# Linear attention and two dense layers on one core: five chunks' keys by tokens turned on TensorE instead of loaded, and the list of operations ordered anew

## The chip, the cores and the metric

The kernel runs on one core of a Trainium2 chip. The metric is the device time of one execution in microseconds (us); the time of the kernel before is the median of three runs.

The engines are named as the profile names them: PE is TensorE's matmuls and PEld its weight loads, DVE is VectorE, ACT is ScalarE, POOL is GpSimd, SP is SyncE, whose queue issues the DMAs.

## The reference

The input is q, k and v of shape (2 batches, 8 heads, 768 tokens, 64 features) and one decay `lam` per head. Attention is linear with a decaying state, in blocks of 64 tokens:

```python
intra = einsum('bhic,bhjc->bhij', qb, kb) * Dmask        # Dmask[i, j] = lam ** (i - j) for i >= j, else 0
intra = einsum('bhij,bhjd->bhid', intra, vb)
inter = einsum('bhid,bhde->bhie', qb * lam_pow, kv_state)
out[:, :, sl] = intra + inter
kv_state = lam_block * kv_state + einsum('bhsd,bhse->bhde', kb * rev_pow, vb)
```

The output becomes x, 1536 tokens by 512. Then come two dense layers of the same sizes (512 to 2048 to 512): `g = elu(x @ w_in)`, `x = g @ w_out`, and with other weights `g = softplus(x @ w_in)`, `out = g @ w_out`. All in float32.

## The kernel before, in words

**Attention.** The kernel takes the tokens in 12 chunks of 128 (two blocks of 64), six per batch. For each chunk it loads two tiles of 512 KB: `qk`, q and k by features (a feature per partition, tokens along the row), and `kv`, k and v by tokens (a token per partition, heads and features along the row). So k is loaded twice, in both layouts. The steps of chunk g, with the names that the planner gives them:

- LQ and LV: the loads (`att_load`, L253, and `att_load_kv`, L267). Chunk 0's q and k come in two DMAs of half the columns (L264), all others in one.
- S: the scores, 32 matmuls of 64x64 weights (`att_s`, L293, the matmul is L308) into two PSUM banks `aps`. SC (L325) multiplies them by the decay mask on DVE.
- KP: the keys by tokens times `kdecay`, in place (`att_prep_k`, L281): one instruction of 128x512 on POOL or DVE (L287), or eight of 128x64 on ACT (L285).
- ST: the chunk's contribution to the state, 16 matmuls of these keys against the values (`att_state`, L383, matmul L389). AD (L395, L397) adds it to the decayed state on DVE, and FD (L402) decays the new state for the next chunk.
- QP: q times its powers (L279). X: the outputs, 48 matmuls, 32 in the first chunk of a batch, where there is no state (`att_x`, L331, matmul L339): first the products with the state, then those of the masked scores with the values. XH and XL (L372, L380) split the result into two parts for the dense layers.

**Dense layers.** Products are made of float32 split in a high and a low part, three matmuls each. The first layer's hidden products are `hps` (L412 to L414) and, for two of the three token tiles of 512, a form with seven products instead of eight (`pa`, `pb`, `pd`, on the same lines); the second product of each layer is `y` (L465). Weights come in 64 tasks of 512 KB (`w_load`, L148) and are split by ACT and DVE (L694 to L713).

**The order of the work.** Nothing is ordered by hand. At build time `build` (L618) makes an `Op` for each step, with the engines it may run on and their costs, a key (its due time, counted from the nominal times of `chunk_at`, L625, plus a shift per kind: KQ, KK, KF, KS, KX, KL) and the operations that it depends on. `schedule` (L504) plays these as a list: a free engine takes the ready operation of the lowest key, and the order in which operations are taken is the order of the program. `NUDGE` (L41) shifts the keys of single operations by number. `Q_ON`, `K_ON` and `F_ON` (L598 to L601) say which engines QP, KP and FD may go to. POOL takes an operation only if at least QUEUE operations wait for DVE and DVE is still busy for PACK times POOL's cost (L574 to L578). TensorE takes from three sequences (attention, first products, second products); HELD and PILE (L560) say how many second products must wait before they go ahead of first ones. `FIRST_LOADS` (L604) is the order of SP's first loads. SHIFT (L592) is the chunk from which the scores use one `aps` pair of banks instead of two; the other pair is then given to the sums `y`, so it sets when second products may begin. From chunk JOIN (L594) on, ST is issued inside X. The four PSUM banks b0 to b3 are shared by ST, by the decay powers and by the first layer's products (`take_bank`, L745).

The program opens with 15 matmuls that keep TensorE at work until the first load lands (L189, L192).

Of the kernel before, what the change touches and what calls it, by code (L numbers as in the profile page):

```python
# [13 lines left out]
AF = mybir.ActivationFunctionType  # L14
# [3 lines left out]
P = 128  # L18
# [20 lines left out]


NUDGE = {  # L41
# [6 lines left out]
}  # L48


# [22 lines left out]
def body(ctx, tc, lamc, attqk, attkv, w1, w2, out):  # L73
# [122 lines left out]
    def swapped(p, e):  # L196
        return e ^ p // 2
# [47 lines left out]
    def powers_out(ps):  # L245
        A.activation(out=qpow.rearrange("q a i -> q (a i)"), in_=ps, func=AF.Copy)

    at = {}

    def early(tag):  # L250
        return xp.tile([P, 2, DM], F32, tag=tag, name="early")

    def att_load(g):  # L253
        if g in (3, 4):
            qk = early(("xl2a", "xl2b")[g - 3])
        elif g in (5, 6):
            qk = tq.tile([P, 2, DM], F32, tag=("t1h", "t1l")[g - 5], name="earlyqk")
        else:
            qk = ap3.tile([P, 2, DM], F32, tag="qk", name="qk")
        if g:  # L260
            nc.sync.dma_start(out=qk, in_=attqk[g])
        else:
            for c in (slice(0, HALF), slice(HALF, DM)):
                nc.sync.dma_start(out=qk[:, :, c], in_=attqk[g].rearrange("p (a i) -> p a i", a=2)[:, :, c])  # L264
        at[g] = [qk[:, 0], qk[:, 1]]

    def att_load_kv(g):  # L267
        if g in (2, 3):
            kv = early(("xh2a", "xh2b")[g - 2])
        elif g in (4, 5):  # L270
            kv = tq.tile([P, 2, DM], F32, tag=("t2h", "t2l")[g - 4], name="earlykv")
        else:
            kv = ap2.tile([P, 2, DM], F32, tag="kv", name="kv")
        nc.sync.dma_start(out=kv, in_=attkv[g])
        at[g] += [kv[:, 0], kv[:, 1]]

    def att_prep(e, g):
        q = at[g][0].rearrange("p (a i) -> p a i", a=NPAIR)
# [1 line left out]

    def att_prep_k(e, g):  # L281
        k = at[g][2].rearrange("p (h d) -> p h d", h=H)
        if e == "A":
            for h in range(H):
                A.activation(out=k[:, h], in_=k[:, h], func=AF.Copy, scale=kdecay[:, h:h + 1])  # L285
        else:
            engines[e].tensor_tensor(out=k, in0=k, in1=kdecay.unsqueeze(2).to_broadcast([P, H, D]), op=ALU.mult)  # L287
# [5 lines left out]
    def att_s(g, ps):  # L293
# [13 lines left out]
                x = x.rearrange("q (a i) -> q a i", a=2)  # L307
            T.matmul(out_, k[r, a:a + 64], x, start=True, stop=True, skip_group_check=True)  # L308

        if g:  # L310
            for late_half in range(2):
                for p0 in range(2):
                    for e in range(2):
                        for p in (p0, p0 + 2):
                            mul(p, e, late_half)
        else:
            for p in range(NPAIR):
                for late_half in range(2):
                    for e in range(2):
                        mul(p, e, late_half)  # L320
        sps[g] = ps

# [162 lines left out]
    def Either(on, key, fn, after=(), gate=None, end=None):  # L485
        return Op(on, key, fn, after, gate, end, True)
# [101 lines left out]
    SLIM = 0.72  # L588
    MM3, SCALAR, SB_V, SB_G, PS_V = 0.68, 0.635, (0.69, True), (1.295, True), (0.69, False)
    PIPE = {"P": 0.0, "A": 0.1, "V": 0.08, "G": 0.04, "S": 0.0}  # L590
    PILE, HELD, QUEUE, PACK = 2.9, 3.9, 1, 0.8
    SHIFT = 10  # L592

    JOIN, CHAIN = 99, 99  # L594
    LATENCY, AHEAD = 2.15, 0.0
    FREE = {"P": 4.6, "A": 2.1, "G": 1.4, "V": 1.65, "S": 0.8}
    FIRST, STEP, ATT = 22.4, 4.71, 3.95
    Q_ON = {"V": (0.69, True)}  # L598
    K_ON = {"A": 2.2, "G": (1.04, True), "V": (0.69, True)}
    F_ON = {"G": (0.62, True)}  # L600
    Q_EARLY, K_EARLY, F_EARLY, EASY = {"V": (0.69, True)}, {"G": (1.04, True)}, {"V": (0.415, True)}, 0  # L601
    KQ, KK, KF, KS, KX, KW, KL = 2, 1.01, 1.37, 0.56, 5.54, -0.91, 15.1
    KT, LATE, RAW_LAG, MARGIN = 0.18, 3.1, 0.69, 0.06
    FIRST_LOADS = [("q", 0), ("v", 0), ("q", 1), ("v", 1), ("q", 2), ("v", 3), ("q", 3), ("v", 2), ("q", 4), 1, ("v", 4), 0, ("q", 5), ("q", 6), ("v", 5)]  # L604

    def lkey(name, key):
        return -90.0 + FIRST_LOADS.index(name) if name in FIRST_LOADS else key

# [9 lines left out]
    def build():  # L618
# [133 lines left out]
        def give_bank(ps):  # L752
            banks[owner[id(ps)]] = True
# [5 lines left out]
        def attention_ops():  # L759
# [18 lines left out]
            for g in range(NCHUNK):  # L778
# [5 lines left out]
                    {"S": ("dma", 2.1 if g == 1 else 1.28)}, lkey(("q", g), k - KL), lambda g=g: att_load(g),  # L784
                    get(("S", old_q), ("X", old_q)))
                O["LV", g] = lv = Op(
                    {"S": ("dma", 1.28)}, lkey(("v", g), k - KL + 2.0), lambda g=g: att_load_kv(g),
                    get(("KP", old_v), ("ST", old_v), ("X", old_v)), lambda g=g: g in at)

                box[g] = aps[g % 2 if g < SHIFT else 0]  # L790
# [4 lines left out]
                else:  # L795
                    O["S", g] = s = pe(0.95, k, lambda g=g: att_s(g, box[g]), here)
                if not last:
                    O["KP", g] = Either(K_ON if g > EASY else K_EARLY, k + KK, lambda e, g=g: att_prep_k(e, g), [lv, ends])

                O["SC", g] = sc1 = Op({"V": (0.97, False)}, k + KS, lambda g=g: att_sc(g), [s, spin, O.get(("X", g - 2))])  # L800

# [831 lines left out]
```

## Time and profile before

| | us |
|---|---|
| median of 3 runs | 558.38 (558.3 to 561.29) |
| profiled execution | 559.15 |
| its span in the profile | 557.4 |
| PE busy in the span | 543.0 (97%) |
| DVE busy | 502.5 (90%) |
| ACT busy | 413.5 (74%) |
| POOL busy | 7.8 (1%) |

The profile is of one execution. Its span runs from the first to the last instruction that the profiler saw; 1.75 us of the execution's time lie around it. Times inside the profile are counted from the start of the span. "PEclk" is the clock that was granted to TensorE as a share of 2.4 GHz; its two levels here are 2.4 and 1.2 GHz. "DMA share" is the busy share of the 16 DMA engines. Matmuls are pipelined, so the duration of a single one is longer than the distance to the next; a group's own duration tells what it takes. A wait in square brackets behind an instruction is the idle time of its engine before it, with what ended it; "issue" means that the profile shows nothing that it waited for.

### The profile page before, as it was taken

What the parts mean: (1) busy time and instruction counts of PE and PEld (TensorE: products, weight loads), DVE (VectorE), ACT (ScalarE), POOL (GpSimd) and SP (SyncE); (2) the same over time, 40 slices, a digit from 0 to 9 for tenths busy, and PEclk for the clock granted to TensorE, in tenths of its full rate; (3) what the DMA queues carried; (4) which work ended last, traced back from release to release, by engine and by line L of the source; (5) the groups of instructions that cost most, each with busy time, mean ns of one, the idle gap of its engine ahead of it and who ended that gap; (6) DMA issues with size and microseconds to landing.
All of it is one profiled execution on the core that took longest, in us unless ns stands there. A gap on an engine that the chain in (4) does not pass through costs nothing.

```text
span 557.4 us, 9041 instructions
## 1 busy us (share of the span) xinstructions
PE 543.0 (97%) x3435; PEld 453.2 (81%) x3435; DVE 502.5 (90%) x907; ACT 413.5 (74%) x775; POOL 7.8 (1%) x14
## 2 busy tenths in 40 slices
PE   7799999999999999999999999999999999999997
PEld 6677788888888888888888888888888888888885
DVE  6689999999669996778998999999999999999895
ACT  3569788778577793657767589999876979697881
POOL 1101000000000000000000000000000000000000
PEclk9899999999999999999999999999999999999999
DMA  8958644012024232301310001122121311221023
GB/s 300 408 182 276 200 133 132 2 38 76 1 76 151 77 102 88 113 2 38 113 54 24 1 1 38 39 81 71 38 76 38 115 38 47 67 79 36 1 94 133
DMA packets 14987, 49.87 MB, mean 89 GB/s; under 512 B 1760, under 2 KB 2272, under 8 KB 14944
## 3 DMA queue, kind: packets, MB, share of 16 engines
q1 hardware_dynamic: 14800, 49.29, 26.0%
q8 instruction: 27, 0.44, 0.4%
q14 instruction: 16, 0.13, 0.1%
q10 hardware_dynamic: 144, 0.01, 0.0%
HBM read 46.15 MB, written 3.15 MB: 88 GB/s over the span
## 4 chain that ended last, share of the span: by engine, by line
PE 87%; DVE 7%; ACT 2%; issue 1%; DMA 1%; SPq 0%; DVEq 0%; ACTq 0%
PE y L465 44%; PE pa L413 5%; PE pa L412 5%; PE pa L414 5%; PE hps L412 3%; PE hps L413 3%; PE hps L414 3%; PE aps L339 3%; PE pd L413 2%; PE pd L414 2%; PE pd L412 2%; DMA qk<-attqk 1%; PE pb L413 1%; PE pb L414 1%; PE pb L412 1%
## 5 line engine op out<-in xcount | busy, mean ns | idle before, releaser
L465 PE MATMUL y<-woh,g 128*128 128x512 f32 x384 | 118.7, 390 | 0.0
L465 PE MATMUL y<-g,woh 128*128 128x512 f32 x384 | 118.5, 390 | 0.0
L992 ACT ACTIVATE g<-v 128x512 fp32r<-128x512 f32 x96 | 60.0, 627 | 38.5 <-PE y L465 33.6
L465 PEld LDWEIGHTS y<-g,woh 128*128 128x128 f32 x384 | 71.9, 188 | 15.0
L465 PEld LDWEIGHTS y<-woh,g 128*128 128x128 f32 x384 | 71.2, 188 | 14.2
L610 DVE TENSOR_TENSOR g<-v,g 128x512 fp32r<-128x512 f32 x96 | 65.5, 686 | 10.3 <-ACT g L992 10.0
L465 PE MATMUL y<-g,wol 128*128 128x512 f32 x192 | 74.7, 389 | 0.0
L465 PE MATMUL y<-wol,g 128*128 128x512 f32 x192 | 74.7, 389 | 0.0
L1343 DVE TENSOR_TENSOR yacc<-y,yacc 128x512 f32<-128x512 f32 x68 | 44.6, 685 | 8.8 <-PE y L465 8.7
L694 ACT ACTIVATE r<-raw 128x512 f32<-128x512 f32 x64 | 42.4, 663 | 5.2 <-DMA raw<-w 3.1
L475 ACT ACTIVATE e<-e 128x512 f32<-128x512 f32 x72 | 45.0, 626 | 0.8
L708 DVE CUSTOM_DVE_ANT_0 r<-r,c 128x1024 uint16<-128x1024 uint16 x64 | 43.8, 684 | 1.3 <-ACT c L698 0.2
L698 ACT ACTIVATE c<-raw 128x512 uint32<-128x512 uint32 x64 | 42.4, 663 | 2.3 <-DVE r L708 2.3
L465 PEld LDWEIGHTS y<-wol,g 128*128 128x128 f32 x192 | 36.0, 188 | 7.5
L465 PEld LDWEIGHTS y<-g,wol 128*128 128x128 f32 x192 | 36.0, 188 | 7.5
L967 ACT ACTIVATE e<-e 128x512 f32<-128x512 f32 x48 | 30.0, 626 | 9.8 <-DVE e L964 9.5
L610 DVE TENSOR_TENSOR e<-e,e 128x512 f32<-128x512 f32 x48 | 32.6, 683 | 2.3 <-ACT e L967 2.1
L964 DVE SCALAR_TENSOR_TENSOR e<-e,e 128x512 f32<-128x512 f32 x48 | 32.7, 683 | 1.3 <-ACT e L958 1.3
L412 PE MATMUL hps<-xh,wih 128*128 128x512 f32 x80 | 31.7, 396 | 0.0
L413 PE MATMUL hps<-xl,wih 128*128 128x512 f32 x80 | 31.2, 390 | 0.0
L414 PE MATMUL hps<-xh,wil 128*128 128x512 f32 x80 | 31.1, 389 | 0.0
L958 ACT ACTIVATE e<-e 128x512 f32<-128x512 f32 x48 | 30.0, 625 | 0.5
(228 smaller groups left out, 1194.2 us busy)
## 6 DMA issues: line engine op xcount, KB each, us to landing
raw<-w SPq DMA_DIRECT2D x64, 512.0 KB, 3.7
kv<-attkv SPq DMA_DIRECT2D x8, 512.0 KB, 5.7
qk<-attqk SPq DMA_DIRECT2D x7, 512.0 KB, 7.7
out<-yacc SPq DMA_DIRECT2D x12, 256.0 KB, 2.1
early<-attqk SPq DMA_DIRECT2D x2, 512.0 KB, 9.6
early<-attkv SPq DMA_DIRECT2D x2, 512.0 KB, 9.7
earlykv<-attkv SPq DMA_DIRECT2D x2, 512.0 KB, 10.6
earlyqk<-attqk SPq DMA_DIRECT2D x2, 512.0 KB, 11.0
```

Of the source, the lines that this page charges most:

```text
L412: T.matmul(ps, wh[:, wo[i]], xa[i], start=(start and i == 0), stop=False, skip_group_check=True)
L413: T.matmul(ps, wh[:, wo[i]], xb[i], start=False, stop=False, skip_group_check=True)
L414: T.matmul(ps, wl[:, wo[i]], xa[i], start=False, stop=(stop and i == n - 1), skip_group_check=True)
L465: T.matmul(yps[m], a, b, start=(begins(key) and i == 0), stop=(ends(key) and i == 2))
L475: A.activation(out=o, in_=a, func=AF.Exp, scale=-1.0)
L610: engines[e].tensor_tensor(out=o, in0=a, in1=b, op=ALU.subtract)
L694: A.activation(out=r, in_=high.bitcast(F32), func=AF.Prelu, scale=2.0 ** -112, alpha=-2.0 ** 32)
L698: A.activation(out=box["c"], in_=box["low"], func=AF.Copy, scale=2.0 ** -29)
L708: V.tensor_tensor(out=ri, in0=ri, in1=box["c"], op=ALU.add)
L964: V.scalar_tensor_tensor(out=e, in0=box["u"], scalar=-1.0, in1=e, op0=ALU.add, op1=ALU.subtract)
L992: A.activation(out=g[:, 0], in_=box["v"], func=AF.Copy)
L1343: V.tensor_tensor(out=y, in0=yps[m], in1=y, op=ALU.add)
```

## The change

- For chunks 0 to 4 (`g < TURN`), the keys by tokens are no longer loaded: `att_load_kv` loads the values alone, 256 KB. The new `att_turn` makes the keys from those by features: 16 matmuls per chunk, each of a 64x64 block of k as weights against the 64x64 identity `ids`, into two PSUM banks. It is an operation of TensorE with S as its dependency, a key of 0.43 after S's, and the condition that at least two of the four shared banks are free. KP of these chunks reads PSUM and writes the tile in SBUF: two instructions of 128x256 on DVE, or eight of 128x64 on ACT, not on POOL. The banks come free when KP has run.
- Chunk 0's q and k are loaded by one DMA, and its scores are issued in the order of the other chunks.
- The planner's numbers are new: where QP, KP and FD may run (POOL now for QP, no longer for KP or FD), the shifts of the keys, HELD, QUEUE and PACK, FIRST and STEP, the order of the first loads, SHIFT from 10 to 8, JOIN from 99 to 8 (so ST of chunks 8 on goes inside X), and all of NUDGE (52 operations shifted before, 71 after).

```diff
 NUDGE = {
-    338: -0.7, 340: -0.4, 344: 0.2, 353: 0.0, 356: 0.9, 360: -5.0, 362: 1.4, 364: 3.1, 373: 0.3, 384: -4.1, 387:
...
+    159: 8.7, 339: 3.1, 344: -9.3, 347: -3.3, 356: -1.1, 361: -0.1, 379: -3.9, 489: -10.1, 500: -2.4, 509: 4.6,
...
-    at = {}
+    at, turned = {}, {}
...
+    TURN = 5
...
-        if g:
-            nc.sync.dma_start(out=qk, in_=attqk[g])
-        else:
-            for c in (slice(0, HALF), slice(HALF, DM)):
-                nc.sync.dma_start(out=qk[:, :, c], in_=attqk[g].rearrange("p (a i) -> p a i", a=2)[:, :, c])
+        nc.sync.dma_start(out=qk, in_=attqk[g])
...
-        nc.sync.dma_start(out=kv, in_=attkv[g])
+        if g < TURN:
+            nc.sync.dma_start(out=kv[:, 1], in_=attkv[g][:, DM:2 * DM])
+        else:
+            nc.sync.dma_start(out=kv, in_=attkv[g])
         at[g] += [kv[:, 0], kv[:, 1]]
+
+    def att_turn(g, ps):
+        k = at[g][1]
+        for half in range(2):
+            for p0 in range(2):
+                for e in range(2):
+                    r = slice(64 * e, 64 * e + 64)
+                    for p in (p0, p0 + 2):
+                        c = 64 * (swapped(p, e) ^ half)
+                        a = P * p + 64 * half
+                        T.matmul(
+                            ps[e][c:c + 64, D * p:D * p + D], k[r, a:a + 64], ids[r], start=True, stop=True,
+                            skip_group_check=True)
...
     def att_prep_k(e, g):
         k = at[g][2].rearrange("p (h d) -> p h d", h=H)
-        if e == "A":
+        if g < TURN:
+            for c, ps in enumerate(turned[g]):
+                if e == "A":
+                    for p in range(NPAIR):
+                        h = 2 * p + c
+                        A.activation(out=k[:, h], in_=ps[:, D * p:D * p + D], func=AF.Copy, scale=kdecay[:, h:h + 1])
+                else:
+                    V.tensor_tensor(
+                        out=k[:, c::2], in0=ps[:, 0:NPAIR * D].rearrange("p (a d) -> p a d", a=NPAIR),
+                        in1=kdecay[:, c::2].unsqueeze(2).to_broadcast([P, NPAIR, D]), op=ALU.mult)
+        elif e == "A":
...
-    PILE, HELD, QUEUE, PACK = 2.9, 3.9, 1, 0.8
-    SHIFT = 10
-    JOIN, CHAIN = 99, 99
+    PILE, HELD, QUEUE, PACK = 2.9, 6.9, 4, 0.0
+    SHIFT = 8
+    JOIN, CHAIN = 8, 99
...
-    FIRST, STEP, ATT = 22.4, 4.71, 3.95
-    Q_ON = {"V": (0.69, True)}
-    K_ON = {"A": 2.2, "G": (1.04, True), "V": (0.69, True)}
-    F_ON = {"G": (0.62, True)}
-    Q_EARLY, K_EARLY, F_EARLY, EASY = {"V": (0.69, True)}, {"G": (1.04, True)}, {"V": (0.415, True)}, 0
-    KQ, KK, KF, KS, KX, KW, KL = 2, 1.01, 1.37, 0.56, 5.54, -0.91, 15.1
-    KT, LATE, RAW_LAG, MARGIN = 0.18, 3.1, 0.69, 0.06
-    FIRST_LOADS = [("q", 0), ("v", 0), ("q", 1), ("v", 1), ("q", 2), ("v", 3), ("q", 3), ("v", 2), ("q", 4), 1, ("v", 4), 0, ("q", 5), ("q", 6), ("v", 5)]
+    FIRST, STEP, ATT = 22.28, 4.76, 3.95
+    Q_ON = {"G": (1.295, True), "V": (0.69, True)}
+    K_ON = {"A": 2.2, "V": (0.69, True)}
+    F_ON = {"V": (0.415, True)}
+    Q_EARLY, K_EARLY, F_EARLY, EASY = {"G": (1.295, True), "V": (0.69, True)}, {"G": (1.04, True)}, {"V": (0.415, True)}, 0
+    KQ, KK, KF, KS, KX, KW, KL = 1.54, -2.34, 1.37, 0.56, 5.54, 1.23, 15.1
+    KN = 0.43
+    KT, LATE, RAW_LAG, MARGIN = 0.84, 3.1, 0.5, 0.09
+    FIRST_LOADS = [("q", 0), ("v", 0), ("q", 1), ("q", 2), ("v", 1), ("v", 3), ("q", 3), ("v", 2), ("q", 4), 1, ("v", 4), 0, ("q", 5), ("q", 6), ("v", 5)]
...
                 if not last:
-                    O["KP", g] = Either(K_ON if g > EASY else K_EARLY, k + KK, lambda e, g=g: att_prep_k(e, g), [lv, ends])
+                    k_on, here, give = K_ON if g > EASY else K_EARLY, [lv, ends], None
+                    if g < TURN:
...
+                        k_on = {e: (0.78, False) if e == "V" else t for e, t in k_on.items() if e != "G"} or {"V": (0.78, False)}
+                        here = here + [pe(0.5, k + KN, turn, [s], lambda: sum(banks.values()) > 1)]
+                    O["KP", g] = Either(k_on, k + KK, lambda e, g=g: att_prep_k(e, g), here, end=give)
```

## Rows read from the trace of the kernel before

**Rows 1.** The page's parts 1 and 3: TensorE's busy time, DMA queue 8 (packets, MB, share).

```profile
PE 543.0 (97%) x3435; PEld 453.2 (81%) x3435; DVE 502.5 (90%) x907; ACT 413.5 (74%) x775; POOL 7.8 (1%) x14
...
q8 instruction: 27, 0.44, 0.4%
```

**Rows 2.** Windows by stage: length, busy us (instructions) of each engine, PEclk, DMA share, GB/s.

```profile
4.83:11.55 6.72, 4.53 (x114) 3.75 (x113) 3.73 (x10) 2.59 (x8) 1.04 (x1) 1.00 1.00 392
11.55:19.36 7.81, 7.30 (x219) 6.25 (x219) 5.56 (x10) 4.57 (x17) 0.62 (x1) 1.00 1.03 410
19.36:21.87 2.51, 0.00 (x2) 0.01 (x2) 1.47 (x3) 2.51 (x8) 1.00 (x1) 1.00 0.99 395
21.87:27.67 5.80, 5.70 (x126) 5.00 (x127) 3.31 (x6) 1.01 (x3) 0.73 (x1) 0.71 1.03 412
27.67:28.91 1.24, 0.00 (x0) 0.00 (x0) 1.24 (x3) 0.98 (x2) 0.00 (x0) 1.00 1.02 403
28.91:30.63 1.72, 1.64 (x55) 1.44 (x55) 1.25 (x3) 0.55 (x2) 0.00 (x0) 1.00 1.04 398
30.63:75.00 44.37, 42.74 (x698) 34.63 (x692) 41.19 (x71) 36.74 (x83) 3.75 (x4) 1.00 0.59 194
75.00:550.00 475.00, 473.68 (x2203) 396.15 (x2203) 438.69 (x786) 363.22 (x659) 0.00 (x0) 1.00 0.19 62
550.00:557.40 7.40, 3.69 (x17) 2.73 (x15) 2.73 (x4) 0.00 (x0) 0.00 (x0) 1.00 0.38 142
```

**Rows 3.** TensorE's timeline, 4.8 to 30 us: start, duration, group [idle before].

```profile
4.83 1.53 PE L308 MATMUL aps<-qk 64*64 64x128 f32 x32
...
7.73 1.40 PE L339 MATMUL aps<-sc,kv 64*64 64x64 f32 x32 [0.34 <-DMA kv<-attkv]
8.94 0.85 PE L308 MATMUL aps<-qk 64*64 64x128 f32 x32
11.55 0.90 PE L308 MATMUL aps<-qk 64*64 64x128 f32 x32 [1.75 <-DMA qk<-attqk]
...
18.80 0.56 PE L389 MATMUL stps<-early 128*64 128x64 f32 x11
21.87 0.39 PE L389 MATMUL stps<-early 128*64 128x64 f32 x5 [2.51 <-issue]
...
27.17 0.50 PE L339 MATMUL aps<-sc,earlykv 64*64 64x64 f32 x9
28.91 1.11 PE L339 MATMUL aps<-sc,earlykv 128*64 128x64 f32 x23 [1.24 <-issue]
```

**Rows 4.** DMA queue 8 in the windows 12 to 33, 19 to 20 and 26 to 27 us.

```profile
q8 instruction: 4, 0.07, 1.2%
...
q8 instruction: 1, 0.02, 6.3%
...
q8 instruction: 1, 0.02, 6.4%
```

**Rows 5.** Groups by line and shape, 0 to 60 us: key and state scaling, state addition, q.

```profile
L285 ACT ACTIVATE kv<-kv,kdecay 128x64 f32<-128x64 f32 x32 | 8.0, 335 | 0.4 <-DMA kv<-attkv 0.4
...
L402 POOL TENSOR_TENSOR faded<-state,qpow 128x256 f32<-128x256 f32 x7 | 6.1, 872 | 40.1 <-DVE state L397 21.4 <-DVE state L395 12.0 <-ACT early L285 6.6
...
L279 DVE TENSOR_TENSOR qk<-qk,qpow 128x512 f32<-128x512 f32 x6 | 4.1, 678 | 0.0
...
L397 DVE TENSOR_TENSOR state<-stps,faded 128x256 f32<-128x256 f32 x7 | 2.9, 415 | 0.1
...
L279 DVE TENSOR_TENSOR early<-early,qpow 128x512 f32<-128x512 f32 x2 | 1.8, 894 | 0.0
...
L287 POOL TENSOR_TENSOR kv<-kv,kdecay 128x512 f32<-128x512 f32 x1 | 1.0, 1044 | 6.4 <-DMA kv<-attkv 6.4
```

**Rows 6.** TensorE's timeline at 52.55 us: the outputs of a chunk, held by q's multiplication.

```profile
52.55 0.67 PE L339 MATMUL aps<-qk,state 64*64 64x128 f32 x16 [0.99 <-DVE qk L279]
```

More of the change, by code (lines that the diff above doesn't have):

```diff
@@ L308, in mul @@
             T.matmul(out_, k[r, a:a + 64], x, start=True, stop=True, skip_group_check=True)
[L310 to L319, printed above, removed]
+        for late_half in range(2):
+            for p0 in range(2):
+                for e in range(2):
+                    for p in (p0, p0 + 2):
                         mul(p, e, late_half)
@@ L786, in attention_ops @@
                 O["LV", g] = lv = Op(
-                    {"S": ("dma", 1.28)}, lkey(("v", g), k - KL + 2.0), lambda g=g: att_load_kv(g),
+                    {"S": ("dma", 0.64 if g < TURN else 1.28)}, lkey(("v", g), k - KL + 2.0), lambda g=g: att_load_kv(g),
                     get(("KP", old_v), ("ST", old_v), ("X", old_v)), lambda g=g: g in at)
@@ L797, in attention_ops, with turn, give @@
                 if not last:
-                    O["KP", g] = Either(K_ON if g > EASY else K_EARLY, k + KK, lambda e, g=g: att_prep_k(e, g), [lv, ends])
+                    k_on, here, give = K_ON if g > EASY else K_EARLY, [lv, ends], None
+                    if g < TURN:
+                        def turn(g=g):
+                            turned[g] = [take_bank("turned") for e in range(2)]
+                            att_turn(g, turned[g])
+                        def give(g=g):
+                            for ps in turned[g]:
+                                give_bank(ps)
+                        k_on = {e: (0.78, False) if e == "V" else t for e, t in k_on.items() if e != "G"} or {"V": (0.78, False)}
+                        here = here + [pe(0.5, k + KN, turn, [s], lambda: sum(banks.values()) > 1)]
+                    O["KP", g] = Either(k_on, k + KK, lambda e, g=g: att_prep_k(e, g), here, end=give)
                 O["SC", g] = sc1 = Op({"V": (0.97, False)}, k + KS, lambda g=g: att_sc(g), [s, spin, O.get(("X", g - 2))])
```

12 rows, old and new, of the table NUDGE are left out of this document.

## The prediction

> **What bounds it now.** I read the page first, then the windows by stage, then TensorE's timeline of the start, then the DMA queues. Everything is set against the profiled execution: 559.15 us, a span of 557.4 us and 1.75 us around it. The median of the three runs shown, 558.38, is 0.77 below, so I subtract that from every sum. About 0.5% (2.8 us) is what a measurement of this kernel can tell from no change, so "faster" means below 555.6 and "slower" above 561.2.
>
> TensorE is busy for 543.0 of 557.4 us [rows 1]. The windows say where the other 14.4 us lie [rows 2]: from 75 to 550 us it is idle for only 475.00 - 473.68 = 1.3 us, from 30.63 to 75 for 1.6, in the tail for 3.7 (last sums and stores, which the change does not touch). The stretch from 4.83 us (the first chunk's scores) to 30.63 (the first matmul of the first layer) holds 6.6 us of idleness: 2.2 + 0.5 + 2.5 + 0.1 + 1.2 + 0.1 over its six windows. One of these windows also ran at a mean granted clock of 0.71 of 2.4 GHz, that is partly at 1.2 GHz, right after TensorE had stood for 2.51 us; against full speed that is 5.80 x 0.29 = 1.7 us lost. So 8.3 us are to be had at the start and hardly anything elsewhere. In all six windows the DMA engines are full (share 0.99 to 1.04).
>
> What are those waits? The timeline [rows 3] names loads for two: 0.34 us for the first keys and values, 1.75 us for chunk 2's q and k. The two longest, 2.51 and 1.24 us, have no releaser. Both fall inside a group whose members share their operands (after 11 of 16 state products, after 9 of 32 output products), and between them lie exactly 5+32+16+48+16+9 = 126 matmuls. Queue 8 carries instructions: 27 packets, 0.44 MB, so 16 KB each; TensorE executes 2 x 3435 = 6870 instructions, 254 for each packet, 127 matmuls with their weight loads [rows 1]. Between 12 and 33 us there are four such packets, one of them at each stop [rows 4]. I read both stops as TensorE standing at the end of a code block whose successor has not come. From stop's end to stop's end it is 28.91 - 21.87 = 7.04 us. Counting 127 back from 19.36 gives 14.75, 7.1 us before 21.87; another 127 back is S(1) at 8.94. So with full DMA engines TensorE gets one block of 127 matmuls per 7 us, while such a block needs only about 7.30/219 x 127 = 4.2 us.
>
> **The change, part by part.**
>
> *Turns.* Five chunks get 16 matmuls each, 64 x 64, as heavy as the second halves of the scores. S(1) does 32 in 0.85 us [rows 3], so a turn is 0.43 us and five are **+2.1**. Lower bound 0, if all lie in load waits; upper bound by code: 80 of 127 matmuls x 7.04 = +4.4. I take 2.1: as long as code paces TensorE, 160 more instructions leave it 80 matmuls behind when transfers thin out, and it makes these up at full speed. A turn waits for what S(g) waits for, and for two free banks. Behind it in TensorE's order stand the state products; banks bind only once layer-one products want one, after 30 us.
>
> The Trainium skill (Runtime: NRT & Kernel Launch, "Instruction fetch mechanics") says code comes in 16 KiB blocks of 256 instructions, fetched while the current one runs, so that crossing a boundary is mostly hidden. The block size agrees with the rows; "mostly hidden" does not for the two stops of 2.51 and 1.24 us. By that rule the waits would be for loads alone; that is the first rival.
>
> *Loads.* Five loads of keys and values shrink from 512 to 256 KB: 1.31 MB, at 403 to 410 GB/s [rows 2] 3.2 us of transfer. Chunk 0's values land 0.64 us earlier, so X(0) and S(1), at the beginning of a code block, move up: **-0.5** (0 to -0.64). Chunk 2's q and k have 768 KB less ahead of them, 1.9 us, and their 1.75 us wait goes; but S(2) lies in the same code block, so what it gains is stood off at the next boundary: 0 in the sum (-1.75 as a bound). The transfers end 3.2 us earlier, near 27.4 us, which is where the second stop begins; I take that stop as gone, **-1.24** (0 to -1.24).
>
> *First load whole.* One issue on SyncE instead of two, nothing late behind it. S(0) ran 1.53 us instead of S(1)'s 0.85, so it waited for the second half inside; whole, it starts later and ends about where it did. 0, bounds -0.5 and +0.5.
>
> *Scaling of keys.* Before: POOL 1.04 us for chunk 0, ACT 8 x 0.335, or DVE. After: ACT as before, or DVE twice 128x256 from PSUM; the nearest row, the state addition from PSUM, takes 0.415 [rows 5], so 0.83. Fades move from POOL (0.87) to DVE at about that 0.415. Five scalings and four fades are 5.8 us on DVE at most; it is idle for 25.8 - 16.6 = 9.2 us in the stretch, so 0. Without that cover the state chain would be late by one 0.83.
>
> *List anew.* Multiplications of q may go to POOL when DVE has four jobs waiting. A DVE row beside POOL averages 894 ns instead of 678 [rows 5]; DVE has 3.2 us of slack between 30.63 and 75, so 0, bound +1. The 0.99 us stop at 52.55, for a q multiplication behind others on DVE [rows 6], should go with new keys: **-1.0** (0 to -1.0). Products that join outputs from chunk 8 are only reordered. With one score bank for chunks 8 to 11, S(g) waits for the split of chunk g-1, while output products may start two chunks earlier; TensorE has both to pick from: 0, at worst +1. From 75 us on the new shifts can win or lose the 1.3 us that stand idle there: 0, bounds -1.3 and +1.3.
>
> Sum: 2.1 - 0.5 - 1.24 - 1.0 = -0.6; 558.5 against the profiled execution, **557.7** against the median. From the bounds, this case reaches from 555.6 to 561.
>
> **Rivals.**
>
> *Loads were the bound all along.* If the code arrives in time once the engines carry less, or if the new order brings boundaries to where TensorE waits anyway, then the start is left with TensorE's own work. All of it is 8.3 us of loss gone against 2.1 of turns: -6.2, 552.2. With half the loss left it is 4.15 - 2.1 = -2.05, 556.3 before later gains and 555.3 with the 1.0 above. I put it at 554.2. For it: the first 0.34 and 1.75 us are loads by name, and everything from chunk 1 on arrives 0.6 to 3.2 us earlier. Against: the two largest stops name no load.
>
> *A third stop, slower.* After the second stop the kernel needs only 55 matmuls to the first long one [rows 2], so the next boundary falls among matmuls of 128x512, where 127 take 27 us (475 us for 2203 from 75 us on); it costs nothing. Eighty more matmuls make it 135, over the 127 of a block: the third boundary falls among the small ones. If the transfers are still full there, the stop is 7.04 - 4.2 = 2.8, and no stop goes: 2.1 - 0.5 + 2.8 = +4.4, 562.8; with 1.7 of half clock after it, 564.5. It is decided by whether the share of the DMA engines is still near 1 when that boundary comes. Against: 3.2 us less transfer.
>
> *It does not do what it says.* The outputs need the values and the q's as before; if keys were never the last to land, no wait goes and only the turns stay. That gives +2.1, 560.5, inside the first case's bounds, and I count it there.
>
> **Chances.** Code pace with the saving eaten, 557.7: 0.45, all of it "same". Loads as the bound, 554.2: 0.38, faster; the queue's 3.2 us is a large saving against 2.1 us of matmuls, and half of these can lie in waits. Third stop, 562.8: 0.17, slower. The range from 553.0 to 562.0 leaves out the end of the second case (0.07) and most of the third (0.11). The first case's own range is 555.6 to 561.
>
> **What would show it.** Right: 3515 matmuls; chunk 2's scores about 2 us earlier; queue 8's packets still some 7 us apart up to 27 us, with stops without a releaser inside groups, the first of them now with less old work done; the first layer-one product within 1.5 us of 30.6. The first rival shows no such stop over 1 us and layer one beginning before 28. The second shows three stops, or a granted clock under 0.8 over more than 6 us, and layer one beginning after 33. Wrong in another way would be idle time of TensorE of over 3 us between 75 and 550 us, or a longer tail: then the list, not the keys, sets the difference.

## The result, and the profile after

The changed kernel takes 564.22 us (median of 5 runs, 563.69 to 564.73). The kernel before takes 560.08 in 5 runs on the same chip, and the ratio of the two sets of runs is 1.0078 with a 95% interval of 1.0054 to 1.0101: slower by 3 to 5.7 us. On another chip, with twelve runs of the kernel before, it came to 1.0088 (1.0075 to 1.0101). The forecast was 557.7 with a range up to 562.0.

| | before | after |
|---|---|---|
| profiled execution, us | 559.15 | 564.41 |
| its span | 557.4 | 562.7 |
| PE busy | 543.0 | 547.6 |
| PE matmuls | 3435 | 3595 |
| MB moved by the DMA engines | 49.87 | 48.58 |

The page's parts 1 and 3 of the kernel after, the lines that answer to [rows 1]:

```profile
PE 547.6 (97%) x3595; PEld 456.5 (81%) x3595; DVE 501.3 (89%) x911; ACT 414.7 (74%) x780; POOL 2.0 (0%) x7
...
q8 instruction: 28, 0.46, 0.3%
```

TensorE executes 160 matmuls more, not the 80 that I had priced, and one more packet of code is fetched. The windows by stage show where the time went; the cuts are at the stops, as in [rows 2]:

```profile
4.83:12.36 7.53, 7.36 (x207) 5.97 (x206) 6.11 (x21) 1.59 (x4) 0.00 (x0) 1.00 1.01 398
12.36:14.27 1.91, 0.00 (x1) 0.00 (x1) 1.17 (x3) 1.35 (x7) 0.00 (x0) 1.00 1.02 403
14.27:17.96 3.69, 3.60 (x126) 3.25 (x127) 1.83 (x3) 2.59 (x10) 0.00 (x0) 1.00 1.01 406
17.96:20.55 2.59, 0.00 (x1) 0.00 (x0) 1.18 (x3) 1.36 (x3) 0.00 (x0) 0.88 1.02 403
20.55:30.44 9.89, 9.71 (x253) 8.66 (x253) 7.19 (x14) 4.27 (x14) 1.28 (x1) 0.69 0.84 324
30.44:31.99 1.55, 0.00 (x0) 0.00 (x0) 1.17 (x3) 1.55 (x7) 0.00 (x0) 1.00 0.00 0
31.99:34.13 2.14, 2.05 (x55) 1.71 (x55) 1.60 (x3) 0.62 (x2) 0.00 (x0) 1.00 0.04 11
34.13:80.00 45.87, 45.23 (x730) 36.14 (x724) 39.84 (x73) 35.18 (x73) 0.00 (x0) 1.00 0.53 185
80.00:130.00 50.00, 49.10 (x224) 39.96 (x221) 48.91 (x94) 41.09 (x75) 0.00 (x0) 1.00 0.20 64
...
400.00:550.00 150.00, 147.97 (x742) 125.84 (x741) 144.26 (x260) 120.67 (x224) 0.00 (x0) 1.00 0.19 62
550.00:562.70 12.70, 8.83 (x39) 6.97 (x38) 6.82 (x11) 1.90 (x3) 0.00 (x0) 1.00 0.28 105
```

The first layer-one product starts at 34.13 us instead of 30.63, and chunk 5's scores (0.9 us), which the kernel before had done by then, are still to come: 4.4 us behind. There are three stops without a releaser, 6.05 us together, against 3.75 before. Between the first two lie 126 matmuls, as between the two stops before; between the second and the third 253, two blocks. The third stop, at 30.44, comes when the DMA engines are empty (share 0.00). The granted clock was 0.69 over 9.89 us, a loss of 3.1 us against 1.7 before.

Summed over these windows, TensorE is idle for 6.6 us between the first scores and the first layer-one product, as long as before (29.30 - 22.72 and 25.80 - 19.17). The stops have taken the place of the waits for data. So the 4.4 us are busy time: 1.4 of half clock, and some 3 us of turns.

After that the list shows in both directions. From the first product to 80 us TensorE is idle for 0.64 us (1.63 up to 75 us before), so the stop at 52.55 [rows 6] is gone: -1.0. From 80 to 550 us it is idle for 0.90 + 2.03 = 2.9 us (1.3 from 75 on before): +1.6. The tail has 3.87 instead of 3.71. Sum: 4.4 - 1.0 + 1.6 + 0.2 = 5.2; the spans differ by 5.3.

TensorE's timeline of the start, which answers to [rows 3]:

```profile
7.91 0.69 PE L291 MATMUL turned<-ids,qk 64*64 64x64 f32 x32
...
11.23 0.69 PE L291 MATMUL turned<-ids,qk 64*64 64x64 f32 x32
11.74 0.61 PE L336 MATMUL aps<-qk 64*64 64x128 f32 x14
14.27 0.54 PE L336 MATMUL aps<-qk 64*64 64x128 f32 x14 [1.91 <-issue]
...
20.55 0.48 PE L411 MATMUL stps<-early 128*64 128x64 f32 x4 [2.59 <-issue]
...
31.99 0.45 PE L411 MATMUL stps<-earlykv 128*64 128x64 f32 x7 [1.55 <-issue]
```

A turn is 32 matmuls and 0.69 us here. A float32 matmul stands in the profile twice: the 16 that the code writes for a turn are 32 in these rows, as the 16 of the scores are 32 and the 8 of `att_state` 16. (The description of the kernel before counts scores, outputs and state products as the profile does, but the turns as the code does.) The group behind the second turn begins 0.51 us after it (11.23 to 11.74), so counted to the next group a turn can take less than 0.69. The waits for loads (0.34 and 1.75 us) are gone, as forecast, and chunk 2's scores begin at 11.74, no earlier than the 11.55 of before.

### The profile page after: what moved, and what is told of

It is laid out like the page before. It is cut to its first block, busy times and chain, and to the rows that moved or that the text cites. A ratio compares the mean times of both kernels' runs of the same rounds, so it can differ in the third digit from the quotient of the medians.

```text
span 562.7 us, 9348 instructions
## 1 busy us (share of the span) xinstructions
PE 547.6 (97%) x3595; PEld 456.5 (81%) x3595; DVE 501.3 (89%) x911; ACT 414.7 (74%) x780; POOL 2.0 (0%) x7
## 2 busy tenths in 40 slices
DMA packets 14588, 48.58 MB, mean 86 GB/s; under 512 B 1744, under 2 KB 1744, under 8 KB 14544
## 4 chain that ended last, share of the span: by engine, by line
PE 94%; DVE 2%; issue 2%; DMA 1%; ACT 0%; DVEq 0%
PE y L487 46%; PE pa L434 5%; PE pa L435 5%; PE pa L436 5%; PE aps L361 4%; PE hps L434 3%; PE hps L435 3%; PE hps L436 3%; PE pd L435 2%; PE pd L436 2%; PE pd L434 2%; PE aps L336 2%; PE pb L435 1%; PE pb L434 1%; PE pb L436 1%
```

## The experiments

Three theories stood against each other. **Code pace**: TensorE gets its code in blocks of 256 instructions, slowly while transfers run, so the turns' instructions cost. **Work**: the turns cost the 5 x 0.69 = 3.5 us that TensorE spends on them. **List**: the new order costs.

**1. Taking the turns out, or putting them alone into the kernel before.** The changed kernel with whole loads and no turns, operation numbers kept so that each shift meets its operation, and chunk 0's keys scaled on DVE as in the changed kernel:

```diff
-    TURN = 5
+    TURN = 0
...
```

> The changed kernel without its turns: the five chunks' keys by tokens are loaded as before (512 KB instead of 256), scaled on ACT or DVE, and the new list, its shifts and its other rules stay. Theory code pace: the turns are 160 of TensorE's matmuls with their loads, 320 instructions, one and a quarter code blocks, so without them the start has two stops without a releaser instead of three, the first layer-one product comes near 30.5 to 31.5 us instead of 34.1, and the time is 560 to 561. Rival work alone: the turns cost what their matmuls take, 5 x 0.69 = 3.5 us, so about 560.7, but with stops as long as in the changed kernel (6.0 us together). Rival new list: the loss is in the order and the shifts, the time stays at 563 or more.

Measured: 1.0133 (1.0117 to 1.0149), slower than the changed kernel. The first product came at 31.28 us, 2.9 earlier, with chunk 5's scores already done. But the list, planned for the turns, came out in another order without them. TensorE's waits in that run's window from 80 to 130 us grew from 0.9 to 3.4 us, 2.34 of them one wait for a sum on ACT. So the run shows that taking the turns out speeds up the start, and nothing of the total. The turns alone in the kernel before, with the old list:

```diff
-        nc.sync.dma_start(out=kv, in_=attkv[g])
+        if g < TURN:
+            nc.sync.dma_start(out=kv[:, 1], in_=attkv[g][:, DM:2 * DM])
...
+                        here = here + [pe(0.5, k + KN, turn, [s], lambda: sum(banks.values()) > 1)]
```

> The kernel before with the turns alone: same list, same rules and shifts, first load in halves, five chunks' keys turned and their loads halved. Theory code pace: as many instructions at the start as the changed kernel, so three stops of 5 us or more together, first layer-one product at 33 to 35, time 3 to 5 us over the kernel before (563 to 565). Rival work alone: +2 to +3.5. Rival new list: the time of the kernel before or less, 558 to 560.

Measured: 1.0161 (1.0143 to 1.0178), +9 us, more than any theory gave. Stops of 1.89, 1.52, 0.84 and 1.49 us, the first product at 35.10, and at 58.47 a wait of 2.28 us for scaled keys on DVE. With turns, the new list is thus the better one: 4.1 to 4.9 us over the kernel before instead of 9. Since the planner makes another order when operations are taken out or added, the order is held fixed from here on, and only what is issued inside an operation changes.

**2. The same order with little code, and with no turns.** The turn as 2 matmuls of 256 columns:

```diff
-        for half in range(2):
...
+        for e in range(2):
+            r = slice(64 * e, 64 * e + 64)
+            T.matmul(
+                ps[e][:, 0:NPAIR * D].rearrange("p (a d) -> p a d", a=NPAIR), k[r, 0:P],
+                ids[r].unsqueeze(1).to_broadcast([64, NPAIR, D]), start=True, stop=True, skip_group_check=True)
```

> The changed kernel with each turn made by 2 matmuls of 256 columns in place of 16 of 64 (4 for 32 as the profile counts them): about the same time on TensorE (2 x 256 columns of float32 for 16 x 64, half the columns, but no cover of two array halves at once: 0.5 to 0.9 us a turn against 0.69), and 280 instructions fewer. It leaves out the turning: every head gets the first head's keys. Theory code pace: the stops stand where the instructions of the kernel before would put them, two instead of three or three with the third among layer-one products, first layer-one product at 30.5 to 32, time 560.5 to 562. Rival work alone: nothing changes, 564 within 1. Rival new list: nothing changes either.

And no matmul at all in the turn's place, the scaling reading `ids`:

> The changed kernel in its own order, without one matmul of the turns: the loads stay halved, the scaling of the keys reads the identity in SBUF instead of the turned keys in PSUM (it leaves out the turning, so the keys are the identity's). Theory code pace: TensorE's instructions at the start are those of the kernel before, so two stops without a releaser in place of three, at the 256-instruction marks of that order; against the kernel with 2 matmuls a turn only the 0.7 us of each turn go, and only where no stop swallows them: 0 to 3.5 us less than its 563.0, so 559.5 to 562.5. Rival work alone: the turns' matmuls (3.5 us) and nothing else, so 560.7 with the stops unchanged at 6 us. If the halved loads are worth the 3.2 us of transfer that they save, the first layer-one product comes 3 us before the 30.6 of the kernel before.

Measured: 1.0065 (1.0043 to 1.0086) and, on another chip, 1.0011 (0.9996 to 1.0027). To divide the loss, all three were run side by side:

> The changed kernel itself, again, so that it stands on one chip and beside the same runs of the kernel before as the two variants that follow. 1.0065 to 1.009 of the kernel before.

> The changed kernel with 2 matmuls of 256 columns a turn, again (TensorE is as long at each turn, 0.70 us for 0.69, with 280 instructions fewer; it leaves out the turning). Theory code pace: 0.3 to 0.5% less than the changed kernel. Theory work: less than 0.15% below it.

> The changed kernel without a matmul of the turns, again (the keys are the identity's). Theory work: 0.5 to 0.65% less than the kernel with 2 matmuls a turn, the 3.5 us that TensorE no longer spends. Theory code pace: within 0.2% of it, since both have nearly the same instructions.

| | turns on TensorE | instructions of the turns | ratio to before (95%) |
|---|---|---|---|
| as changed | 5 x 0.69 us | 320 | 1.0088 (1.0075 to 1.0101) |
| 2 matmuls a turn | 5 x 0.70 us | 40 | 1.0066 (1.0049 to 1.0082) |
| none | 0 | 0 | 1.0031 (1.0019 to 1.0043) |

The step for the code is 0.22% (1.2 us; the intervals just overlap), the step for the work 0.35% (2.0 us; they don't), and 0.31% (1.7 us) is left without any turn. Neither theory alone holds. Three limits belong to this table. The kernel without turns had come to 1.0011 on the other chip, so what is left without turns is 0.1 to 0.3%. Taking the turn out also takes out the scaling's wait for it, and the scaling reads SBUF instead of PSUM; the runs do not separate this from the time of the matmuls. And without turns TensorE stands for 3.6 us in waits for DVE between 4.83 and 30.16 us, so part of the turns had filled such waits.

The timeline of the kernel with 2 matmuls a turn, in the run beside the other two, shows what the code does: two stops, 3.68 us, and none between the second and layer one:

```profile
8.02 0.70 PE L286 MATMUL turned<-ids,qk 64*128 64x256 f32 x4
...
16.08 0.87 PE L356 MATMUL aps<-sc,kv 128*64 128x64 f32 x14 [1.39 <-issue]
...
22.93 0.26 PE L331 MATMUL aps<-early 64*64 64x64 f32 x1 [2.29 <-issue]
...
32.87 0.50 PE L429 MATMUL hps<-xh,wih 128*128 128x512 f32 x1
```

The changed kernel's second profile, from this run, shows how far the stops vary from one execution to the next. Its windows at the stops:

```profile
19.56:20.46 0.90, 0.00 (x2) 0.00 (x0) 0.86 (x3) 0.90 (x2) 0.00 (x0) 1.00 1.05 419
20.46:24.64 4.18, 3.79 (x127) 3.15 (x126) 3.73 (x8) 2.17 (x7) 0.00 (x0) 1.00 1.03 411
24.64:26.64 2.00, 0.01 (x1) 0.00 (x0) 0.77 (x2) 1.30 (x7) 0.00 (x0) 1.00 0.99 397
26.64:30.29 3.65, 3.55 (x126) 3.20 (x127) 2.92 (x6) 0.84 (x3) 1.28 (x1) 1.00 0.53 210
30.29:30.47 0.18, 0.00 (x2) 0.00 (x1) 0.18 (x2) 0.18 (x2) 0.00 (x0) 1.00 0.00 0
```

With the first, again of 1.91 us, these are four stops, one at each count of 126 or 127 matmuls, 4.99 us together. The first layer-one product comes at 32.61 and the span is 562.2, against 34.13 and 562.7 in the first profile. The counts are the same, the lengths aren't. Queue 8 shows what ends a stop. These are its rows of the first profile, in the windows 11.7 to 11.8, 18.1 to 18.2 and 29.6 to 29.7 us, where the packets ahead of the three stops start:

```profile
q8 instruction: 1, 0.02, 67.6%
...
q8 instruction: 1, 0.02, 66.8%
...
q8 instruction: 1, 0.02, 60.0%
```

The stops end at 14.27, 20.55 and 31.99, each 2.3 to 2.6 us after its packet starts, the last one too, though the other transfers are over by then. In the second profile packets start at 12.0, 18.1, 24.2 and 28.1, and the four stops end 2.4 to 2.5 us later. So a stop is long when its packet starts late, or when TensorE has used up the block before it early. What sets the start of a packet was not settled.

The second profile also tells which terms of the first belong to that execution alone. Its start, the stretch to 80 us and the one behind it:

```profile
4.83:32.61 27.78, 21.32 (x642) 18.11 (x641) 19.74 (x47) 13.28 (x43) 1.28 (x1) 0.94 0.87 341
32.61:80.00 47.39, 45.73 (x739) 36.43 (x733) 41.10 (x74) 35.06 (x73) 0.00 (x0) 1.00 0.53 179
80.00:550.00 470.00, 467.16 (x2173) 390.44 (x2173) 432.71 (x777) 363.04 (x660) 0.00 (x0) 1.00 0.19 61
```

At the start TensorE is idle for 6.5 us and loses 1.7 to the clock, both as in the kernel before, and it is 2.9 us behind (2.0, and chunk 5's scores): that is what the turns take. Up to 80 us it is idle for 1.7 us, no less than before, 0.94 of it in two waits for DVE, one of them again for a multiplication of q. From 80 to 550 us it is idle for 2.8 us, +1.5, and the tail is 0.2 longer. That makes 4.6; the spans differ by 4.8. So the extra half clock and the gain at 52.55 us are not to be counted on, while the turns and the waits behind 80 us are in both profiles.

**3. What the halved loads are worth.** The kernel before in its own order, the five loads halved, no turning:

```diff
+        if g < 5:
+            nc.sync.dma_start(out=kv[:, 1], in_=attkv[g][:, DM:2 * DM])
...
+        x = ids.unsqueeze(1).to_broadcast([P, H, D]) if g < 5 else k
```

> The kernel before in its own order, with the five loads of keys and values halved and no turning: the scaling of the keys reads the identity in SBUF (it leaves out the keys by tokens of five chunks). TensorE's instructions are those of the kernel before. It measures what 3.2 us less transfer are worth where they cost nothing. Theory loads as the bound: 2 to 3.2 us faster than the kernel before, first layer-one product near 28. Theory code pace and chain of data: the stops stay at the same matmuls (behind 11 of chunk 3's state products, behind 9 of chunk 4's output products), only the 1.75 us wait for chunk 2's q and k goes, and most of it is stood off at the next stop: within 1 us of the kernel before.

Measured: 0.9990 (0.9972 to 1.0008), no difference that can be measured. Its timeline:

```profile
10.40 0.90 PE L312 MATMUL aps<-qk 64*64 64x128 f32 x32 [0.89 <-DMA qk<-attqk]
...
14.37 0.99 PE L343 MATMUL aps<-sc,kv 128*64 128x64 f32 x19 [0.33 <-issue]
...
21.21 0.39 PE L393 MATMUL stps<-early 128*64 128x64 f32 x5 [2.30 <-issue]
...
27.50 1.11 PE L343 MATMUL aps<-sc,earlykv 128*64 128x64 f32 x23 [1.32 <-issue]
...
29.22 0.50 PE L416 MATMUL hps<-xh,wih 128*128 128x512 f32 x1
```

Both stops stand behind the same 11 and 9 matmuls as in [rows 3] and are about as long as before, though they end 0.7 and 1.4 us earlier. A third, of 0.33 us, stands 126 matmuls ahead of the first: the boundary that the prediction had counted back to 14.75, which cost nothing in the kernel before. 3.2 us of transfer saved give 1.4 us in this profiled execution and about 0.5 in the median; the interval allows 1.6 at most. In this order, then, the loads were not the bound.

**4. What is left: the list.** This kernel and the one without turns have the same instructions of TensorE at the start and the same loads; they differ in the list (and in the first load, and the two profiles in the clock: 1.000 and 0.993 on average, 3.9 us over the span, so the spans are not compared). Their windows from 80 to 130 and from 400 to 550 us, first the old list, then the new:

```profile
80.00:130.00 50.00, 50.00 (x222) 41.44 (x221) 49.64 (x94) 38.92 (x71) 0.00 (x0) 1.00 0.18 62
...
400.00:550.00 150.00, 148.70 (x731) 125.46 (x730) 142.62 (x256) 116.48 (x213) 0.00 (x0) 1.00 0.18 60
```

```profile
80.00:130.00 50.00, 49.19 (x216) 40.08 (x215) 49.78 (x96) 41.31 (x74) 0.00 (x0) 1.00 0.21 67
...
400.00:550.00 150.00, 147.96 (x736) 125.49 (x735) 144.27 (x259) 119.58 (x221) 0.00 (x0) 1.00 0.19 61
```

TensorE idles 2.85 us in these with the new list and 1.30 with the old: +1.55, and the waits are the changed kernel's, whether turns run or not. In the changed kernel they are, from 80 to 130 and from 400 to 550 us:

```profile
PE pa L434 <- DVE v L1167: 0.8, 1, 0.8
```

```profile
PE y L487 <- DVE wol L633: 1.2, 1, 1.2
PE za L434 <- DVE v L1240: 0.8, 1, 0.8
```

All three are for DVE, which is 98 and 96% busy there. Which shift or rule makes each was not tried.

**5. Moving the block boundaries.** If the stops are ends of code blocks, more instructions ahead of all work must move them by as many matmuls. Five kernels issue more, smaller matmuls at the opening:

```diff
-        for n, times in ((256, 5), (384, 2)):
+        for n, times in ((32, 64), (256, 1), (384, 1)):
```

> The changed kernel with the opening matmuls cut smaller: 64 of 32 columns in place of 5, so 59 matmuls (118 instructions) more ahead of the first scores, in the time when TensorE waits for its first load anyway. Theory code blocks: each stop moves by 59 matmuls back in the order of work (the first from the 14th of chunk 2's scores to the 3rd or so of chunk 0's state products, the second from the 12th of chunk 2's state products to the first output products of chunk 1); the time stays within 1.5 us of the changed kernel's, since the pace of the blocks is the same. Rival, the stops are waits for data that the profile does not name: they stay behind the same matmuls.

```diff
-        for n, times in ((256, 5), (384, 2)):
+        for n, times in ((256, 2),):
...
+        for i in range(34):
+            T.matmul(ps[:64, :64], zero[:64, :64], zero[:64, :64], start=True, stop=True)
```

> The changed kernel with 68 small matmuls (64x64) in place of 5 of the opening ones, 63 matmuls or 126 instructions more ahead of the first scores, for about the same time on TensorE (earlier than 5.5 us). Theory code blocks: each stop moves 63 matmuls back in the order of work: the first from inside chunk 2's scores to the beginning of chunk 0's state products, the second from inside chunk 2's state products to the state part of chunk 1's outputs, the third from inside chunk 4's state products into chunk 3's outputs; the time stays within 1.5 us of the changed kernel's. Rival, waits for data that the profile does not name: the stops stay behind the same matmuls.

> The kernel before with the same 63 matmuls more at its opening. Theory code blocks: the first stop moves from inside chunk 3's state products to the end of chunk 2's outputs, the second from inside chunk 4's outputs into chunk 3's; the time stays within 2 us of the kernel before. Rival, waits for unnamed data: the stops stay where they were, behind 11 of chunk 3's 16 state products and behind 9 of chunk 4's output products.

These three went wrong as timings: the small matmuls took far longer than planned (68 into one part of the array 7.4 us), so the first scores began at 10.65 us in the last two and later in the first. Ratios: 1.0281 (1.0264 to 1.0297), 1.0217 (1.0187 to 1.0247), 1.0052 (1.0029 to 1.0075). As tests of place they hold. In the kernel before with 63 matmuls more, the stops moved to where the count puts them:

```profile
24.32 0.33 PE L341 MATMUL aps<-sc,early 64*64 64x64 f32 x3 [0.51 <-issue]
...
30.59 0.33 PE L341 MATMUL aps<-early,state 64*64 64x128 f32 x3 [1.83 <-issue]
```

The first is now before the last 3 of chunk 2's outputs: from there to the old place lie 3 + 16 + 32 + 11 = 62 matmuls. The second is behind 11 of the 16 products with the state in chunk 3's outputs: from there to the old place lie 5 + 32 + 16 + 9 = 62. Waits for data would have stayed behind the same matmuls. The same with the small matmuls spread over four parts of the array, so that they end at about 5.4 us, and with half as many:

```diff
+        for i in range(34):
+            r, c = 64 * (i % 2), 64 * (i // 2 % 2)
+            T.matmul(
+                (ps, ps2)[i % 2][c:c + 64, 64 * (i % 8):64 * (i % 8) + 64], zero[r:r + 64, :64], zero[r:r + 64, :64],
```

> The kernel before with 68 small matmuls over four parts of the array in place of five of the opening ones, 63 matmuls more, done by about 5.2 us. Theory code blocks: the first stop moves to the end of chunk 2's outputs, the second into the state part of chunk 3's; the time stays within 1.5 us of the kernel before, since a block still takes 6 to 7 us to come. If the place of the boundaries matters, this can be the faster kernel by up to 2 us, where the stops fall on waits for data.

> The kernel before with 36 small matmuls in place of three of the opening ones, 33 matmuls more, done by about 5 us. Theory code blocks: the first stop moves into chunk 3's scores, the second into chunk 3's outputs, each 33 matmuls back; the time stays within 1.5 us of the kernel before.

Measured: 1.0025 (1.0009 to 1.0041) and 1.0012 (0.9988 to 1.0035); the stops moved as counted, in the first of them to

```profile
18.91 0.33 PE L345 MATMUL aps<-sc,early 64*64 64x64 f32 x3 [0.16 <-issue]
...
25.46 0.48 PE L345 MATMUL aps<-early,state 64*64 64x128 f32 x3 [2.11 <-issue]
```

the very places of the slow opening. No place of the boundaries tried came out faster than that of the kernel before.

The count holds across all kernels. The profiles show 40 stops without a releaser that are longer than 0.15 us and lie between the first scores and 46 us. Counted from the program's first matmul, each of them stands behind 220 to 221, 346 to 349, 472 to 474 or 599 to 602 matmuls, whatever the kernel, and each ends 2.3 to 2.8 us after a packet of queue 8 starts.

**6. Fewer instructions, as the same result.** Turns of 12 matmuls, one of 64x128 weights for the four heads whose halves lie in order:

```diff
+                if not swapped(p, e):
+                    T.matmul(
+                        ps[e][:, D * p:D * p + D], k[r, P * p:P * p + P], ids[r], start=True, stop=True, skip_group_check=True)
```

> The changed kernel with each turn made by 12 matmuls instead of 16 (24 for 32 as the profile counts them): the four heads whose halves lie in order need one matmul of 64x128 weights instead of two of 64x64. Same result, 40 matmuls and 80 instructions fewer over the five turns. Theory work (the turns cost what TensorE spends on them): 0.17 us a turn, 0.9 us less than the changed kernel. Theory code pace: the 80 instructions are a third of a code block, up to 2 us less if the third stop goes, 0.5 to 2. Rival: nothing, since 64x128 weights hold both halves of the array and cost twice.

Measured: 1.0168 (1.0131 to 1.0205), slower. Its profiled execution was its fastest, 565.02; the three others took 569.3 to 570.0. The clock tells them apart: it was granted at 0.986 to 0.988 on average in the three and at 0.999 in the profiled one, 6 to 7 us more lost in the span, which covers the 4 to 5 us by which they are longer. Why it fell there stays open, since only the one has a profile. In it a turn takes 2.25 us, from 8.11 to 10.36, because the groups of the two shapes follow each other by 0.26 to 0.37 us:

```profile
8.11 0.43 PE L288 MATMUL turned<-ids,qk 64*128 64x64 f32 x2
8.48 0.33 PE L294 MATMUL turned<-ids,qk 64*64 64x64 f32 x4
8.74 0.43 PE L288 MATMUL turned<-ids,qk 64*128 64x64 f32 x2
...
10.36 1.40 PE L363 MATMUL aps<-sc,kv 64*64 64x64 f32 x32
...
33.90 0.50 PE L436 MATMUL hps<-xh,wih 128*128 128x512 f32 x1
```

That is 7.8 us more on TensorE than in the changed kernel, yet the first layer-one product comes at 33.90 (34.13), there is no stop without a releaser, and the granted clock is 1.00 throughout the start. The packets of queue 8 start at 12.8, 18.8, 24.3 and 28.7 us, much as in the changed kernel, but TensorE uses up its blocks so slowly that none comes late. In this execution, then, 7.8 us of work took the place of 6.05 of stops and 3.1 of half clock, which fits a start that is paced by its code.

## Why the prediction was wrong, step by step

The mechanism at the start was right, and three terms failed: the turns were priced about 1.1 us too low, the 1.74 us for earlier transfers did not come, and the list, put at 0 from 75 us on, cost 1.5 to 1.6 there.

- **That code paces the start: right.** Wherever a profile shows two stops they lie 125 to 127 matmuls apart, or twice that, and they move with the count of instructions (experiment 5), as waits for data would not. So the Trainium skill's "mostly hidden" (Runtime: NRT & Kernel Launch, "Instruction fetch mechanics") does not hold for this stage, where three crossings cost 6.05 us; its block of 256 instructions does.
- **The turns, +2.1: mis-sized.** I counted 16 matmuls a turn from the code and priced them by rows in which each matmul of the code stands twice. It is 32 matmuls, 0.69 us, 3.45 for five. The runs give 2.0 us for this work and 1.2 for its code, 3.2 together, and the second profile 2.9 at the start.
- **The second stop gone, -1.24, and -0.5 for an earlier beginning: wrong.** They followed from transfers that end 3.2 us earlier. Transfers did end earlier (share 0.00 at the third stop), but with 320 instructions more one more boundary fell among the small matmuls. The stops grew by 2.3 us, about what the waits for data had taken, so nothing of the idle time was won. Nor did anything begin earlier: chunk 0's turn stands ahead of its outputs, and chunk 1's scores came at 9.83 us instead of 8.94. Even without turns the halved loads gave 0.1%, at most 0.28% (experiment 3). The last stop comes with empty DMA engines in both profiles of the changed kernel; it ends 2.3 to 2.4 us after its packet starts, as other stops do, so less transfer does not take every stop away.
- **The wait for chunk 2's q and k, 0 in the sum: right.** It went, and it was worth nothing. But the sign given for it, chunk 2's scores about 2 us earlier, did not show: two turns and chunk 0's state products stand ahead of them, and the block ended 14 matmuls into them.
- **The list, -1.0 and otherwise 0: wrong in its second half.** The 0.99 us stop went in the first profile; in the second two waits for DVE, 0.94 us together, stand in the same stretch, so the -1.0 was not safe either. The 1.3 us of idleness from 75 us on became 2.9, and +1.6 was beyond the bound of 1.3 that I gave for that stretch, and just under the 3 us that I gave as the sign that the list sets the difference.
- **Scaling, first load, POOL at 0: right as far as can be seen.** DVE is idle for 9 us of the 29 at the start, and the first scores take 1.56 us for 1.53. This holds with the turns in place; without them TensorE does wait for DVE there (experiment 2). The row "beside POOL", 894 ns, was misread: it is the mean of two, 682 and 1106 ns, and POOL was at work beside both. The term stood at 0, so nothing hung on it.
- **The rivals.** The third stop, with a chance of 0.17, is what came, with all its signs: three stops, a granted clock of 0.69 over 9.89 us, layer one after 33. That its price of +4.4 equals the 4.4 us at the start of the first profile is luck: the terms are others (more work, a shorter stop of 1.55 instead of 2.8, more half clock, no waits for loads), and the second profile has 2.9. Its condition, a full DMA share at the third boundary, held in the second profile (2.00 us at a share of 0.99) and not in the first, where the third boundary was passed without a stop at a clock of 0.69 and the fourth had the stop. "Loads as the bound", with 0.38 and a gain of 4 to 6 us, is excluded by experiment 3 for the old order; in the new one the stops that it wanted gone are there.

Put together with what was measured: turns +3.2, list +2.3 (1.0031 without turns against 0.9990 for the halved loads under the old list), loads -0.5, which makes 5.0. The three are steps from one ratio to the next, so that they add up to the 4.9 us of that chip is no check of them; with 1.0011 for the kernel without turns, the list would be 1.2. The terms read from the second profile, 2.9 of turns and 1.5 of waits behind 80 us, are independent of these and say the same. The medians differ by 4.1 us on the first chip, where the ratio makes 4.4.

## What to carry to other kernels

Before pricing an added operation by rows of a profile, count an existing operation of the same code in those rows: in float32 one matmul of the code is two there, with two weight loads. A saved transfer is worth what is left when it costs nothing to save, which one run with the saving and without its price shows; here it was nothing that could be measured. A stage of many tiny matmuls can be bound by their number, so a change that swaps bytes for instructions goes the wrong way there, and a planner's order tuned for one set of operations has to be compared with the order held fixed.

## What the runs showed of the hardware that was not expected

- While loads fill the DMA engines, 256 instructions of TensorE come once in 6 to 7 us (from stop's end to stop's end 7.04 before, 6.28 after). TensorE goes on 2.3 to 2.8 us after the packet of its next block starts, in all 40 stops, also when nothing else moves any more, as at 30.44 to 31.99.
- 68 small float32 matmuls (34 in the code) into one part of the array and one place in PSUM took 7.4 us, 0.109 each; spread over four parts and over two banks they took 1.9, 0.028 each. The runs do not separate the part of the array from the place in PSUM.
- Groups of 64x64 and of 64x128 weights hardly overlap: the 12 matmuls that change between them took 2.25 us, the 16 of one shape 0.69.
- The kernel with turns of 12 matmuls took 565.02 us at a mean granted clock of 0.999 and 569.25 to 569.96 at 0.986 to 0.988.
